# Half-size PSUM tiles, a reordered stage schedule and a fixed matmul order in a long FFT convolution

## The chip, the cores and the metric

The kernel runs on one core of one Trainium2 chip. The metric is device time in microseconds (us), here of that one core. Each kernel was run several times; medians of those runs are quoted, and a ratio comes with a 95% interval. A run is called *slow* when it is over 1.5% above the fastest run of the same kernel, else *fast*; ratios use fast runs only. A time is about 1.8 us longer than the span that the profile of the same run shows (396.82 us and 395.0 us for the kernel before).

Names of engines: PE is the matrix engine, ACT the scalar engine, DVE the vector engine, POOL the general-purpose one, SP the one that mostly issues DMAs. PSUM is the memory that matmuls write into; an *eviction* is the instruction, here on ACT or DVE, that reads a PSUM tile and so frees it. The *granted clock* of PE is the share of its full clock that the profile shows as granted: 1.00 is full, and PE is called *cold* where it is near 0.5 and *warm* where it is near 1.

## The reference

```python
x = A_q
g = sigmoid((x * gate_w).sum(-1, keepdims=True))
# branch a: 4-tap shift convolution of k, times v, then a long convolution by FFT
kv = k_shift * v                                   # S=2048, D=640
y  = irfft(rfft(pad(kv)) * rfft(pad(ssm_k)))[:S]   # padded to 4096
a  = q * (y + kv * ssm_D)
# branch b: sliding attention, 32 heads of 20, 8 keys at a distance of 2, then @ wo
out = g * a + (1 - g) * b
```

## The kernel before: the parts that matter

The kernel does three things one after the other: projections, attention (branch b, which leaves `(1-g)*b` in a scratch buffer), and the FFT stage (branch a). The change touches the last two. The FFTs are written as matmuls with constant matrices, in two steps each way, and the 160 channels of a partition are worked through in four groups, `g` = 0 to 3:

| stage | PE writes | who evicts, into what |
|---|---|---|
| `u_s1`, `h_s1` | 10 small or 5 large `pa` tiles each | ACT casts to `Am` |
| `h_s2` | 6 `pb` tiles | DVE adds `Dg`, giving `Hs`; then two copies give `Hsw` |
| `u_s2` | 6 `pb` tiles | ACT casts to `Up`; then two large DVE products `Vp = Up*Hsw`, `Up = Up*Hs` |
| `inv_s1` | `pa` tiles | ACT casts to `Cm` |
| `inv_s2` | `pa` tiles | DVE multiplies into `a_lin`; POOL adds `b_lin` |

```python
pp = tile_pool(name="af_ps", bufs=2, space=PSUM)
...
# after the loads of the FFT stage: one large multiply
nc.vector.tensor_tensor(a_lin[:], a_lin[:], g_lin[:].unsqueeze(2).to_broadcast([128, 64, 160]), ALU.mult)
...
def s1_stage(X_lin, g):
    ...
        nil = min(4, IL - il0)
        pa = pp.tile([128, 2, 512], F32, name="pa", tag="pa")      # 1024 columns, ring of 2
        for l in range(nil): nc.tensor.matmul(pa[...], lhsT=X_lin[...], rhs=F1bd[:, :], ...)
        evac(Am[:, :, :, :, il0:il0 + nil], src)                   # nc.scalar.copy
...
fwd_u_s1(0)
fwd_h(0)                                                           # h_s1 and h_s2
fwd_u_s2(0)
for g in range(NG):
    if g + 1 < NG: fwd_u_s1(g + 1)
    inv_s1(g)
    if g + 1 < NG: fwd_h(g + 1)
    inv_s2(g)
    if g + 1 < NG: fwd_u_s2(g + 1)
```

When the kernel is built, a scheduler orders the instructions of each engine by readiness, unless instructions carry an *issue-order token*: those with the same token keep the order in which they were written. The kernel before has no such token in its FFT stage, and what it executes is not what is written: in the group that is read below, PE's `inv_s2` matmuls begin at 311.9 us, before the first one of `h_s2` (312.9), and are then spread among them, although `inv_s2(g)` is called after `fwd_h(g + 1)`.

The softmax here doesn't subtract the row's maximum and nothing guards it: scores larger than these inputs give would overflow.

## Time and profile before

| | us |
|---|---|
| median of 4 runs when the prediction was made | 392.98 (390.76 to 396.82) |
| projections, to | 124 |
| attention, to | 233 |
| FFT stage, to the end of the span | 395 |

First the page of the profile: busy time, share of the span, and instructions of each engine. No engine is full over the whole span, but the three parts have different limits, so this line decides nothing.

```profile
PE 265.1 (67%) x3958; PEld 181.3 (46%) x3958; DVE 244.4 (62%) x304; ACT 179.2 (45%) x230; POOL 101.7 (26%) x102
```

The view of windows divides the FFT stage at the ends of the `Up` products of groups 1 to 3. Columns: window, its length, busy time and instructions of PE, weight loads, DVE, ACT, POOL; then the granted PE clock, the DMA share and GB/s.

```profile
262.80:299.30 36.50, 23.70 (x504) 20.05 (x504) 30.28 (x17) 19.02 (x22) 12.08 (x6) 0.87 0.51 111
299.30:333.50 34.20, 23.56 (x504) 20.09 (x504) 19.90 (x17) 19.12 (x22) 12.34 (x7) 0.90 0.01 2
...
367.80:395.00 27.20, 10.78 (x208) 10.20 (x208) 3.24 (x6) 4.93 (x6) 10.36 (x13) 0.69 0.42 98
```

In the steady group of 34.20 us PE is busy for 23.56, DVE for 19.90, ACT for 19.12. No engine is full there either. What does fill the group is seen in the chain of waits: the work that ended last, followed backwards. Columns: start, duration, what (a cut of that same group).

```profile
295.68 3.63 DVE Up L256
...
302.99 1.02 ACT Cm L191
...
308.12 3.77 ACT Am L191 x4
313.50 4.35 DVE Hs L236 x4
...
318.41 1.46 DVE Hs L236 x2
...
320.47 1.49 DVE Hsw L239
321.97 2.31 DVE Hsw L240
...
326.33 3.60 DVE Vp L255
329.95 3.63 DVE Up L256
```

From one `Up` product (ends at 299.3) to the next (333.5) the chain passes through inverse stage 1, the `Am` of h, the `Hs` adds, the copies to `Hsw`, and the two products. The engines take turns.

At the start of the stage stands the large multiply of `a_lin`. DVE's timeline (start, duration, engine, line, operation, tiles, count):

```profile
268.62 10.83 DVE L178 TENSOR_TENSOR a_lin<-a_lin,g_lin 128x10240 bf16<-128x10240 bf16 x1 [5.83 <-DMA a_lin<-in_A_q_dram]
279.36 2.21 DVE L236 TENSOR_TENSOR Hs<-pb,Dg 128x960 bf16<-128x960 f32 x2
281.49 0.65 DVE L299 TENSOR_TENSOR a_lin<-pa,a_lin 128x480 bf16<-128x480 f32 x1
...
295.68 3.62 DVE L256 TENSOR_TENSOR Up<-Up,Hs 128x5120 bf16<-128x5120 bf16 x1
```

It starts when its load lands and runs ahead of all `Hs` adds of group 1. In attention, the line that the change moves to another engine is this group (busy, mean ns of one, idle before):

```profile
L419 DVE TENSOR_SCALAR fin<-op,omg 128x640 bf16<-128x640 f32 x16 | 14.1, 881 | 7.4 <-PE op L416 7.2
```

### The profile page before, as it was taken

The numbers are of one execution on the slowest core, as the hardware profiler recorded it, in microseconds if no ns is written. First come the engines' busy times: TensorE is split into PE (matmuls) and PEld (weight loads), VectorE is DVE, ScalarE is ACT, GpSimd is POOL, SyncE is SP. The second block draws the span as 40 slices with busy tenths as digits, with TensorE's granted clock in tenths as the row PEclk, the third lists the DMA queues.
The fourth block names the chain that finished last, engine by engine and source line by source line (L and its number), as shares of the span: only waits on it lengthen the run. The fifth ranks groups of instructions, "written<-read, shape, count | busy, mean of one in ns | idle before, by whom it ended". The sixth has DMA issues, their size and how long they took to land.

```text
span 395.0 us, 8971 instructions
## 1 busy us (share of the span) xinstructions
PE 265.1 (67%) x3958; PEld 181.3 (46%) x3958; DVE 244.4 (62%) x304; ACT 179.2 (45%) x230; POOL 101.7 (26%) x102
## 2 busy tenths in 40 slices
PE   0599999749541787786968566656666774772730
PEld 0365555324130555465545334545556563672630
DVE  0241095899689879788687623558993297079230
ACT  1025545423371747657374236648084644823310
POOL 5019702091003600000000043000263048017263
PEclk9999999987855559597577989669896998898695
DMA  8935998583351911010000149999300000000037
GB/s 230 264 98 95 161 189 174 114 151 66 76 135 35 201 34 51 2 51 22 33 18 20 50 134 266 298 198 286 45 2 2 2 3 2 0 3 2 2 78 189
DMA packets 26375, 37.36 MB, mean 95 GB/s; under 512 B 15424, under 2 KB 21204, under 8 KB 25824
## 3 DMA queue, kind: packets, MB, share of 16 engines
q1 hardware_dynamic: 21104, 19.62, 20.7%
q0 software_dynamic: 5232, 17.17, 20.0%
q8 instruction: 31, 0.51, 0.5%
q14 instruction: 8, 0.07, 0.1%
HBM read 26.26 MB, written 5.25 MB: 80 GB/s over the span
## 4 chain that ended last, share of the span: by engine, by line
PE 22%; DVE 18%; ACT 10%; SPq 6%; issue 5%; DMA 2%; POOL 2%; POOLq 0%; ACTq 0%; DVEq 0%
PE op L416 7%; SPq L176 6%; ACT ET L453 6%; PE sc L447 4%; DVE Hs L236 4%; PE O L469 4%; DVE Up L256 3%; DVE Vp L255 3%; DMA a_lin<-in_A_q_dram 2%; ACT Cm L191 2%; PE pa L270 2%; DVE a_lin L299 2%; ACT Am L191 2%; PE tr L488 2%; PE pa L272 2%
## 5 line engine op out<-in xcount | busy, mean ns | idle before, releaser
L453 ACT ACTIVATE ET<-sc 128x912 bf16<-128x912 f32 (+1 forms) x80 | 64.1, 854 | 49.2 <-PE sc L447 38.1
L300 POOL TENSOR_TENSOR a_lin<-a_lin,b_lin 128x480 bf16<-128x480 bf16 (+1 forms) x24 | 43.2, 1819 | 97.4 <-DVE a_lin L299 97.4
L369 PE MATMUL pj<-xT,W 128*128 128x512 bf16 x200 | 49.8, 405 | 10.3 <-ACT stg L372 10.3
L454 DVE TENSOR_TENSOR ET<-ET,band 128x912 bf16<-128x912 bf16 (+1 forms) x80 | 45.2, 567 | 8.7 <-ACT ET L453 7.9
L191 ACT CAST Am<-pa 128x1024 bf16<-128x1024 f32 x40 | 37.4, 1039 | 18.4 <-PE pa L201 12.9
L447 PE MATMUL sc<-q,k 20*128 20x114 bf16 x576 | 31.0, 252 | 20.9 <-ACT ET L453 20.0
L270 PE MATMUL pa<-MU,Up 128*128 128x128 bf16 x160 | 28.0, 270 | 21.8 <-DVE Up L256 19.9
L236 DVE TENSOR_TENSOR Hs<-pb,Dg 128x960 bf16<-128x960 f32 (+1 forms) x24 | 23.6, 1036 | 30.4 <-PE pb L221 30.4
L219 PE MATMUL pb<-Am,Gre 64*128 64x80 bf16 x512 | 26.5, 208 | 15.2 <-DVE Hs L236 7.1
L369 PEld LDWEIGHTS <-W 128*128 128x128 bf16 x200 | 20.2, 102 | 35.6 <-issue 15.8
L372 ACT CAST stg<-pj 128x512 bf16<-128x512 f32 x40 | 22.6, 588 | 30.5 <-PE pj L369 18.9
L416 PE MATMUL op<-wo,oT 128*128 128x512 bf16 (+1 forms) x160 | 33.1, 362 | 3.0 <-DVE fin L419 3.0
L191 ACT CAST Cm<-pa 128x1024 bf16<-128x1024 f32 (+1 forms) x24 | 19.7, 875 | 29.5 <-PE pa L272 29.5
L253 ACT CAST Up<-pb 128x960 bf16<-128x960 f32 (+1 forms) x24 | 19.3, 886 | 29.7 <-issue 27.5
L469 PE MATMUL O<-VW,ET 128*128 128x21 bf16 x576 | 21.8, 177 | 13.0 <-DVE o_S L478 12.6
L221 PEld LDWEIGHTS <-Gim 64*128 64x128 bf16 x512 | 22.3, 102 | 17.5 <-issue 17.2
L270 PEld LDWEIGHTS <-Up 128*128 128x128 bf16 x160 | 20.3, 127 | 20.9 <-DVE Up L256 12.2
L399 ACT CAST VW<-psv 128x640 bf16<-128x640 f32 x18 | 12.6, 699 | 37.3 <-PE psv L397 37.3
L447 PEld LDWEIGHTS <-k 20*128 20x128 bf16 x576 | 16.6, 106 | 25.4 <-issue 20.5
L272 PE MATMUL pa<-MV,Vp 128*128 128x128 bf16 x160 | 28.1, 271 | 0.0
L469 PEld LDWEIGHTS <-ET 128*128 128x128 bf16 x576 | 19.1, 101 | 17.3 <-issue 12.9
L221 PE MATMUL pb<-Am,Gim 64*128 64x80 bf16 x512 | 26.7, 208 | 0.0
(75 smaller groups left out, 490.9 us busy)
## 6 DMA issues: line engine op xcount, KB each, us to landing
h_lin<-in_A_v_dram POOLq DMA_DIRECT2D x4, 640.0 KB, 16.3
h_lin<-in_A_ssm_k_dram POOLq DMA_DIRECT2D x8, 320.0 KB, 6.3
b_scr<-fin SPq DMA_DIRECT2D x16, 160.0 KB
W<-in_B_wqkv_dram SPq DMA_DIRECT2D x3, 800.0 KB
kh<-in_A_k_dram POOLq DMA_DIRECT2D x12, 190.0 KB, 13.9
q<-stg SPq DMA_DIRECT2D x28, 80.0 KB
k<-stg SPq DMA_DIRECT2D x28, 80.0 KB
Him<-ca_Him POOLq DMA_DIRECT2D x1, 2048.0 KB, 19.0
```

The lines of the kernel that those rows point to most:

```text
L191: nc.scalar.copy(dst, src)
L221: nc.tensor.matmul(o, lhsT=Gim[rows, j1, :], rhs=Am[rows, j1, 1, :, :].rearrange("p q l -> p (q l)"), start=False, stop=True, tile_positio ...
L236: nc.vector.tensor_tensor(Hs[:, :, :, j0:j0 + nj, :], view, Dgv.unsqueeze(3).to_broadcast([128, 2, IL, nj, 4]), ALU.add)
L270: nc.tensor.matmul(o, lhsT=Up[:, c2, il, :, :].rearrange("p j q -> p (j q)"), rhs=MU[:, :], start=True, stop=False, skip_group_check=True)
L272: nc.tensor.matmul(o, lhsT=Vp[:, c2, il, :, :].rearrange("p j q -> p (j q)"), rhs=MV[:, :], start=False, stop=True, skip_group_check=True)
L300: nc.gpsimd.tensor_tensor(reg, reg, breg, ALU.add)
L369: nc.tensor.matmul(ps[:], lhsT=W[:, dt, which, 128 * ft:128 * ft + 128], rhs=xT[:, dt, HALO + 512 * sc:HALO + 512 * sc + 512], start=(dt = ...
L416: nc.tensor.matmul(op[:, n0:n1], lhsT=oT[:, ft, HALO + 128 * sb:HALO + 128 * sb + 128], rhs=wo[:, ft, n0:n1], start=(ft == 0), stop=(ft == ...
L447: nc.tensor.matmul(sc[:, hh, bb * BP:bb * BP + BP], lhsT=k32[32 * h4:32 * h4 + DH, t, kc:kc + 128], rhs=q32[32 * h4:32 * h4 + DH, t, qc:qc ...
L453: nc.scalar.activation(dst, src, ACT.Exp, scale=SCALE)
L454: nc.vector.tensor_tensor(dst, dst, band[:].unsqueeze(1).unsqueeze(1).to_broadcast([128, 2, nbb, BP]), ALU.mult)
L469: nc.tensor.matmul(O[:, slot * 21:slot * 21 + 21], lhsT=ET[:, h4, bb, :], rhs=VW[:, b, h, :], start=True, stop=True, skip_group_check=True)
```

## The change

The intent is a deeper pipeline: more and smaller PSUM tiles, so that evictions start sooner, and the transform of h one group ahead, so that `Hsw` is ready when `Up` needs it. Five things change:

1. `pa` tiles have 512 columns and a ring of four (four buffers that are used in turn), instead of 1024 and two.
2. The stages are called in another order.
3. Every matmul of the FFT stage carries one issue-order token, so PE executes them as written.
4. In the last group the adds of `b_lin` run on DVE, and the output is stored at rows 24, 48, 60 and 64, the last store from ACT's queue too.
5. `fin` in attention moves from DVE to ACT.

```diff
+        def mm(*args, **kwargs):
+            inst = nc.tensor.matmul(*args, **kwargs)
+            tc.stamp_issue_order_token(inst.ins, "fft_pe")
+            return inst
 ...
-                nil = min(4, IL - il0)
-                pa = pp.tile([128, 2, 512], F32, name="pa", tag="pa")
+                nil = min(2, IL - il0)
+                pa = pp.tile([128, 512], F32, name="pa", tag="pa", bufs=4)
 ...                                  # the same in inv_s1 and inv_s2; all matmuls become mm(...)
-                    nc.gpsimd.tensor_tensor(reg, reg, breg, ALU.add)
+                    (nc.vector if g == NG - 1 else nc.gpsimd).tensor_tensor(reg, reg, breg, ALU.add)
 ...
-        fwd_u_s1(0)
-        fwd_h(0)
-        fwd_u_s2(0)
+        fwd_u_s1(0); fwd_h_s1(0); fwd_h_s2(0); fwd_u_s2(0)
+        if NG > 1:
+            fwd_u_s1(1); fwd_h_s1(1); fwd_h_s2(1)
         for g in range(NG):
-            if g + 1 < NG:
-                fwd_u_s1(g + 1)
             inv_s1(g)
             if g + 1 < NG:
-                fwd_h(g + 1)
+                fwd_u_s2(g + 1)
             inv_s2(g)
-            if g + 1 < NG:
-                fwd_u_s2(g + 1)
+            if g + 2 < NG:
+                fwd_u_s1(g + 2); fwd_h_s1(g + 2); fwd_h_s2(g + 2)
 ...
-            nc.vector.tensor_scalar(fin[:], op[:, 0:D], omg[:, sb:sb + 1], None, ALU.mult)
+            nc.scalar.activation(fin[:], op[:, 0:D], ACT.Copy, scale=omg[:, sb:sb + 1])
```

More of the change, by code (lines that the diff above doesn't have):

```diff
@@ L196, in s1_stage @@
             while il0 < IL:
-                nil = min(4, IL - il0)
-                pa = pp.tile([128, 2, 512], F32, name="pa", tag="pa")
+                nil = min(2, IL - il0)
+                pa = pp.tile([128, 512], F32, name="pa", tag="pa", bufs=4)
                 for l in range(nil):
                     i = IL * g + il0 + l
-                    nc.tensor.matmul(pa[:, l // 2, 256 * (l % 2):256 * (l % 2) + 256],
+                    mm(pa[:, 256 * l:256 * l + 256],
                                      lhsT=X_lin[:, i, :, :].rearrange("p c n -> p (c n)"), rhs=F1bd[:, :],
                                      start=True, stop=True, skip_group_check=True)
-                src = pa[:].rearrange("p b (w m) -> p (b w) m", w=2)[:, 0:nil, :].rearrange("p l (q j r) -> p j r q l", q=4, j=32)
+                src = pa[:, 0:256 * nil].rearrange("p (l q j r) -> p j r q l", l=nil, q=4, j=32)
                 evac(Am[:, :, :, :, il0:il0 + nil], src)
@@ L218, in s2_stage @@
                         o = pb[:, c2, 80 * jj:80 * jj + 80]
-                        nc.tensor.matmul(o, lhsT=Gre[rows, j1, :], rhs=Am[rows, j1, 0, :, :].rearrange("p q l -> p (q l)"),
+                        mm(o, lhsT=Gre[rows, j1, :], rhs=Am[rows, j1, 0, :, :].rearrange("p q l -> p (q l)"),
                                          start=True, stop=False, tile_position=(64 * c2, 0), skip_group_check=True)
-                        nc.tensor.matmul(o, lhsT=Gim[rows, j1, :], rhs=Am[rows, j1, 1, :, :].rearrange("p q l -> p (q l)"),
+                        mm(o, lhsT=Gim[rows, j1, :], rhs=Am[rows, j1, 1, :, :].rearrange("p q l -> p (q l)"),
                                          start=False, stop=True, tile_position=(64 * c2, 0), skip_group_check=True)
@@ L227, in a_fft, with fwd_h_s1, fwd_h_s2 @@
         st = {}
-        def fwd_h(g):
-            Am_h = s1_stage(h_lin, g)
+        def fwd_h_s1(g):
+            st[("Amh", g)] = s1_stage(h_lin, g)
+        def fwd_h_s2(g):
+            Am_h = st.pop(("Amh", g))
             Hs = pl.tile([128, 2, IL, 32, 4], BF, name="Hs", tag="Hs")
@@ L264, in inv_s1 @@
                 while il0 < IL:
-                    nil = min(8, IL - il0)
-                    pa = pp.tile([128, 2, 512], F32, name="pa", tag="pa")
+                    nil = min(4, IL - il0)
+                    pa = pp.tile([128, 512], F32, name="pa", tag="pa", bufs=4)
                     for l in range(nil):
                         il = il0 + l
-                        o = pa[:, l // 4, 128 * (l % 4):128 * (l % 4) + 128]
-                        nc.tensor.matmul(o, lhsT=Up[:, c2, il, :, :].rearrange("p j q -> p (j q)"), rhs=MU[:, :],
+                        o = pa[:, 128 * l:128 * l + 128]
+                        mm(o, lhsT=Up[:, c2, il, :, :].rearrange("p j q -> p (j q)"), rhs=MU[:, :],
                                          start=True, stop=False, skip_group_check=True)
-                        nc.tensor.matmul(o, lhsT=Vp[:, c2, il, :, :].rearrange("p j q -> p (j q)"), rhs=MV[:, :],
+                        mm(o, lhsT=Vp[:, c2, il, :, :].rearrange("p j q -> p (j q)"), rhs=MV[:, :],
                                          start=False, stop=True, skip_group_check=True)
-                    src = pa[:].rearrange("p b (w m) -> p (b w) m", w=4)[:, 0:nil, :].rearrange("p l (n r) -> p n r l", r=2)
+                    src = pa[:, 0:128 * nil].rearrange("p (l n r) -> p n r l", l=nil, r=2)
                     evac(Cm[:, :, :, c2, il0:il0 + nil], src)
@@ L284, in inv_s2 @@
             while n0 < 64:
-                nn = min(24, 64 - n0)
-                pa = pp.tile([128, 2, 512], F32, name="pa", tag="pa")
+                nn = min(12, 64 - n0)
+                pa = pp.tile([128, 512], F32, name="pa", tag="pa", bufs=4)
                 for k_ in range(nn):
                     n2 = n0 + k_
-                    o = pa[:, k_ // 12, 40 * (k_ % 12):40 * (k_ % 12) + 40]
-                    nc.tensor.matmul(o, lhsT=Hre[:, n2, :], rhs=Cm[:, n2, 0, :, :].rearrange("p c l -> p (c l)"),
+                    o = pa[:, 40 * k_:40 * k_ + 40]
+                    mm(o, lhsT=Hre[:, n2, :], rhs=Cm[:, n2, 0, :, :].rearrange("p c l -> p (c l)"),
@@ L291, in inv_s2 @@
                                      start=True, stop=False, skip_group_check=True)
-                    nc.tensor.matmul(o, lhsT=Him[:, n2, :], rhs=Cm[:, n2, 1, :, :].rearrange("p c l -> p (c l)"),
+                    mm(o, lhsT=Him[:, n2, :], rhs=Cm[:, n2, 1, :, :].rearrange("p c l -> p (c l)"),
                                      start=False, stop=True, skip_group_check=True)
-                for bq in range((nn + 11) // 12):
-                    m = min(12, nn - 12 * bq)
-                    yv = pa[:, bq, 0:40 * m].rearrange("p (n c l) -> p n c l", n=m, c=2)
-                    reg = a4[:, n0 + 12 * bq:n0 + 12 * bq + m, :, IL * g:IL * g + IL]
-                    breg = b4[:, n0 + 12 * bq:n0 + 12 * bq + m, :, IL * g:IL * g + IL]
+                if True:
+                    m = nn
+                    yv = pa[:, 0:40 * m].rearrange("p (n c l) -> p n c l", n=m, c=2)
+                    reg = a4[:, n0:n0 + m, :, IL * g:IL * g + IL]
+                    breg = b4[:, n0:n0 + m, :, IL * g:IL * g + IL]
@@ L299, in inv_s2 @@
                     nc.vector.tensor_tensor(reg, yv, reg, ALU.mult)
-                    nc.gpsimd.tensor_tensor(reg, reg, breg, ALU.add)
-                if g == NG - 1:
+                    (nc.vector if g == NG - 1 else nc.gpsimd).tensor_tensor(reg, reg, breg, ALU.add)
+                n0 += nn
+                if g == NG - 1 and n0 in (24, 48, 60, 64):
+                    w0 = {24: 0, 48: 24, 60: 48, 64: 60}[n0]
                     for cq in range(4):
-                        eng = (nc.sync, nc.gpsimd)[cq % 2]
-                        dst = outf[:, 160 * cq:160 * cq + 160].rearrange("(a b) c -> a b c", b=64)[:, n0:n0 + nn, :]
-                        eng.dma_start(dst, a_lin[32 * cq:32 * cq + 32, n0:n0 + nn, :])
@@ L306, in inv_s2 @@
-                n0 += nn
-        fwd_u_s1(0)
-        fwd_h(0)
-        fwd_u_s2(0)
+                        eng = (nc.sync, nc.gpsimd, nc.scalar)[cq % 3] if n0 == 64 else (nc.sync, nc.gpsimd)[cq % 2]
+                        dst = outf[:, 160 * cq:160 * cq + 160].rearrange("(a b) c -> a b c", b=64)[:, w0:n0, :]
+                        eng.dma_start(dst, a_lin[32 * cq:32 * cq + 32, w0:n0, :])
+        fwd_u_s1(0); fwd_h_s1(0); fwd_h_s2(0); fwd_u_s2(0)
+        if NG > 1:
+            fwd_u_s1(1); fwd_h_s1(1); fwd_h_s2(1)
```

## The prediction

> **What bounds it now.** The span (395.0 us, one profiled run of 396.82 against a median of 392.98) has three parts: projection to 124 us, attention to 233, the FFT stage to 395. The change touches the last two. By the windows view no engine is full in the FFT stage: from 299.3 to 333.5 PE is busy 23.6 of 34.2 us, DVE 19.9, ACT 19.1. The chain of waits shows why: one group is a serial chain that repeats every 34.2 us (Up products end at 299.3, 333.5, 367.8): inverse stage 1 on a PE that restarts at half clock 7.6; four or five Am evictions 5.2; Hs adds, Hsw copies and a_lin multiplies on DVE about 13; Vp and Up 7.2; handoffs.
>
> **What the change does.** The instruction order shows PE work pinned in program order; no matmul is added or removed.
> - Evictions of 128x1024 become 128x512. The trace has 1039 ns against 599. The Trainium skill (ScalarE: Activation LUTs, "What ACT_TABLE_LOAD costs") gives 186 ns + 0.833 per element, overlapping by 93: 0.52 us per 512 against 0.95, and the trace agrees (0.92 between starts). Ten Am tiles (9.3 us) become twenty (10.4); Cm 4.9 becomes 5.2. ACT pays about 1.4 us a group.
> - A ring of four small tiles instead of two large lets the first eviction start earlier, 0.4 us per stage.
> - New order: h is transformed a group ahead, so Hsw leaves the chain. But u and h evictions now run back to back inside it, and their PSUM tiles wait for a_lin multiplies, which DVE runs only after Vp and Up. New chain per group, walked by hand: Am 10.4, Hs until PE may go on 4.5, Cm 5.8, Up evictions 4.9, a_lin/Vp/Up 8.3, handoffs 0.8: about 34.7 against 34.2. **The pipeline is relabelled, not shortened.**
> - Start: the a_lin load lands at 268.6 and the 10.8 us DVE multiply after it now stands behind three Hs adds of group 1 and holds up PE, which has inverse stage 1 of group 0 still to do. I expect Up of group 1 about 3 us later.
> - Tail: 512-wide tiles bring the first last-group multiply about 0.9 us sooner after Up; the adds move from POOL (1.1 us each, plus handoff) to DVE (estimated 0.33 from 2.82 us per 5120 elements). But 2.6 MB of output at the 230 GB/s seen takes 11 us, so the end follows the first store: gain 1 to 2 us.
> - fin (883 ns on DVE, 16 times) becomes an ACT activation, estimated 0.81 us (same page, pointer scale). Where op, fin, op alternate, DVE is full (2.8 us per step against 2.2 without fin), so attention may gain 1 to 4 us.
>
> **Sum.** FFT stage +1 to +4 from order and eviction overhead, tail -1 to -2, attention -1 to -4: about -2.5 us, 390.5 us. Range 383 to 397. Chances: faster by 2% 0.22, within 2% 0.70, slower 0.08.
>
> **What would show it.** Time between ends of Up products: 33 to 36 us if right; 30 or less if stages overlap better than I think. ACT should idle 7 to 9 us per group, waiting on PE behind a_lin. The large a_lin multiply should start near 270 minus any attention gain. PE should begin inverse stage 1 warm in groups 1 and 2 (54 ns between matmuls, not 105; skill, TensorE: Matmul & The Clock Gate, "What's actually happening"). Attention windows should be 105 to 108 us instead of 109.
>
> **What would make it wrong.** PE staying cold through the eviction-bound stages (+2 us a group); POOL adds no longer colliding with Vp and Up (3.6 against 2.8 us), which would save up to 1.5 us a group; ACT, about 60% busy in attention, delaying exp behind fin; the output DMA ending sooner.

## The result and the profile after

| | before | after |
|---|---|---|
| median, us | 393.76 (16 runs, 390.76 to 399.39) | 402.79 (11 runs, 400.11 to 406.46) |
| ratio of fast runs | | 1.0225 [1.0186, 1.0263] |
| profiled run: span, mean clock | 395.0, 0.825 | 401.0, 0.786 |

The ratio is the mean time of one kernel's fast runs over the mean of the other's fast runs of the same rounds, so it is not quite the ratio of the two medians. The changed kernel is slower by 2.25%, which is 8.9 us of the 393.76; that it is slower is clear of the noise, that it is slower by 2% is not, as the interval reaches down to 1.0186. The time lies outside the predicted range.

The profile of before fell in a run called slow, for being over 1.5% above the fastest run. So the kernel before was profiled once more, later (run before_again, below; a single run). Its FFT stage agrees with the first profile: 34.0 and 34.1 us between `Up` products against 34.2 and 34.3. In the comparison by stage I use before_again.

| us after the last `fin` (end of attention) | before_again | after | after takes longer by |
|---|---|---|---|
| end of the `Up` product of group 0 | 29.3 | 30.0 | 0.7 |
| of group 1 | 66.2 | 69.9 | 3.7 so far |
| group 1 to 2 | 34.0 | 35.5 | 1.5 |
| group 2 to 3 | 34.1 | 36.1 | 2.0 |
| group 3 to the first output store | 12.9 | 11.0 | -1.9 |
| first store to the end | 14.6 | 15.7 | 1.1 |
| end | 161.7 | 168.2 | 6.5 |
| length of attention | 106.7 | 107.5 | 0.8 |

Attention is counted here from the start of its first `o_S` multiply on DVE to the end of the last `fin`. So 6.5 of the 8.9 us are placed in the FFT stage. The rest is not placed: in this pair of profiles, whose spans differ by 8.3 us, it is 0.8 us of attention and 1.1 us before it, and both are within the scatter. The projection part, which no kernel touches, ends anywhere between 123.0 and 126.8 us in the sixteen profiles, and attention between 106.3 and 107.5 us later; a single pair of profiles can't resolve 2 us there.

The page of after and its windows, cut at the same events. The steady group has grown from 34.20 to 35.60 and 36.10 us although DVE has less to do, ACT only a little more and PE the same matmuls, and the granted clock is 0.79 and 0.78 instead of 0.90 and 0.85.

```profile
PE 274.6 (68%) x3958; PEld 183.8 (46%) x3958; DVE 228.6 (57%) x294; ACT 194.7 (49%) x302; POOL 92.2 (23%) x97
```

```profile
262.80:302.60 39.80, 20.20 (x476) 17.52 (x476) 26.63 (x15) 14.41 (x25) 6.24 (x2) 0.72 0.48 101
302.60:338.20 35.60, 25.16 (x504) 20.08 (x504) 18.05 (x18) 19.97 (x36) 11.05 (x7) 0.79 0.01 2
338.20:374.30 36.10, 25.82 (x504) 20.65 (x503) 17.84 (x17) 20.24 (x36) 10.94 (x7) 0.78 0.01 2
374.30:401.00 26.70, 10.19 (x208) 10.02 (x208) 6.82 (x16) 5.42 (x10) 9.23 (x12) 0.69 0.45 100
```

The chain of waits of this trace reaches back only to 382.5 us, so the group has to be read from timelines. ACT's, where the bracket is the idle time before the instruction and what ended it:

```profile
290.86 4.83 ACT L261 CAST Up<-pb 128x960 bf16<-128x960 f32 x6
303.95 1.12 ACT L196 CAST Am<-pa 128x512 bf16<-128x512 f32 x2 [8.27 <-PE pa L190]
305.24 9.20 ACT L196 CAST Am<-pa 128x512 bf16<-128x512 f32 x18 [0.17 <-PE pa L190]
321.54 4.99 ACT L196 CAST Cm<-pa 128x512 bf16<-128x512 f32 x10 [7.10 <-PE pa L190]
326.32 4.87 ACT L261 CAST Up<-pb 128x960 bf16<-128x960 f32 x6
```

This is the whole group on one engine. All `Am` together take 10.49 us (303.95 to 314.44), then ACT waits 7.10, `Cm` takes 4.78 until the first `Up`, `Up` takes 4.87, and then it waits 8.27 again before the next group. The sum is 35.5 us, the measured distance between groups. The group is a serial chain again, with two holes. DVE's timeline shows what stands in them:

```profile
268.36 3.39 DVE L244 TENSOR_TENSOR Hs<-pb,Dg 128x960 bf16<-128x960 f32 x3 [5.53 <-PE pb L190]
271.66 10.81 DVE L178 TENSOR_TENSOR a_lin<-a_lin,g_lin 128x10240 bf16<-128x10240 bf16 x1
282.40 2.61 DVE L244 TENSOR_TENSOR Hs<-pb,Dg 128x960 bf16<-128x960 f32 x3
...
296.19 2.81 DVE L263 TENSOR_TENSOR Vp<-Up,Hsw 128x5120 bf16<-128x5120 bf16 x1
...
299.49 3.17 DVE L264 TENSOR_TENSOR Up<-Up,Hs 128x5120 bf16<-128x5120 bf16 x1
302.58 2.00 DVE L307 TENSOR_TENSOR a_lin<-pa,a_lin 128x480 bf16<-128x480 f32 x4
```

- The hole of 8.27 us: after the last `Up` eviction DVE does the two long products and only then most of the `a_lin` multiplies, which free the `pa` tiles of `inv_s2`. PE has `u_s1` of the next group behind them in its fixed order, so ACT gets its first `Am` of the next group only at 303.95 us, when the last run of `a_lin` multiplies (from 302.58) has begun to free tiles.
- The hole of 7.10 us: PE is in `h_s2`, where ACT has nothing to do, and `inv_s1`, which would give ACT its `Cm` work, is written after it.
- At the start, the large multiply has slipped behind three of the six `Hs` adds. While it runs, two of the other three `pb` tiles stand full and PE waits 10.81 us to write the sixth (the line below); `inv_s1` of group 0 is written after `h_s2` of group 1, and the first `Cm` comes at 285.06 us, after ACT has been idle for 17.78.

```profile
283.60 0.25 PE L190 MATMUL pb<-Am,Gre 64*128 64x80 bf16 x2 [10.81 <-DVE Hs L244]
```

The PE clock in the same group, from the windows between the events on ACT (`Am`; from `Am` to `Cm`; `Cm`):

```profile
303.95:314.45 10.50, 7.58 (x38) 4.39 (x37) 0.63 (x2) 10.33 (x20) 3.35 (x4) 0.82 0.01 2
314.45:321.50 7.05, 6.21 (x140) 5.46 (x140) 5.96 (x6) 0.00 (x0) 0.00 (x0) 0.52 0.01 2
321.50:326.30 4.80, 4.80 (x120) 4.70 (x118) 3.02 (x3) 4.76 (x10) 0.00 (x0) 1.00 0.00 0
```

`h_s2` runs at a clock of 0.52; just before it PE, which waits for evictions there, had a pause of 1.6 us. `inv_s1` begins cold too, at 320.42 us: its first ten matmuls stand 105 ns apart, the later ones 55 ns. While ACT evicts `Cm`, the clock is 1.00 in this group. In the next group 32 matmuls of `inv_s1` stand 105 ns apart.

In attention, `fin` is now on ACT and takes 793 ns:

```profile
L426 ACT ACTIVATE fin<-op,omg 128x640 bf16<-128x640 f32 x16 | 12.7, 793 | 28.1 <-PE op L423 19.2 <-issue 6.5 <-ACT ET L460 2.4
```

### The profile page after: what moved, and what is told of

It is laid out like the page before. It is cut to its first block, busy times and chain, and to the rows that moved or that the text cites. A ratio compares the mean times of both kernels' runs of the same rounds, so it can differ in the third digit from the quotient of the medians.

```text
span 401.0 us, 9049 instructions
## 1 busy us (share of the span) xinstructions
PE 274.6 (68%) x3958; PEld 183.8 (46%) x3958; DVE 228.6 (57%) x294; ACT 194.7 (49%) x302; POOL 92.2 (23%) x97
## 5 line engine op out<-in xcount | busy, mean ns | idle before, releaser
L376 PE MATMUL pj<-xT,W 128*128 128x512 bf16 x200 | 49.2, 401 | 10.8 <-ACT stg L379 10.8
L308 POOL TENSOR_TENSOR a_lin<-a_lin,b_lin 128x480 bf16<-128x480 bf16 (+1 forms) x18 | 32.8, 1854 | 102.5 <-DVE a_lin L307 102.5
L190 PE MATMUL pb<-Am,Gre 64*128 64x80 bf16 x512 | 32.6, 233 | 27.1 <-DVE Hs L244 14.7
L196 ACT CAST Am<-pa 128x512 bf16<-128x512 f32 x80 | 41.1, 728 | 17.5 <-PE pa L190 17.5
L190 PEld LDWEIGHTS <-Gim 64*128 64x128 bf16 x512 | 27.9, 119 | 31.8 <-issue 31.7
L196 ACT CAST Cm<-pa 128x512 bf16<-128x512 f32 x40 | 21.0, 613 | 42.8 <-PE pa L190 42.8
L190 PE MATMUL pb<-Am,Gim 64*128 64x80 bf16 x512 | 33.2, 235 | 0.1
L307 DVE TENSOR_TENSOR a_lin<-pa,a_lin 128x480 bf16<-128x480 f32 (+1 forms) x24 | 13.3, 591 | 28.9 <-PE pa L190 28.9
L190 PEld LDWEIGHTS <-Gre 64*128 64x128 bf16 x512 | 28.7, 119 | 1.1 <-issue 0.8
L476 PEld LDWEIGHTS <-ET 128*128 128x128 bf16 x576 | 19.2, 102 | 18.2 <-issue 12.7
L426 ACT ACTIVATE fin<-op,omg 128x640 bf16<-128x640 f32 x16 | 12.7, 793 | 28.1 <-PE op L423 19.2
L190 PE MATMUL pa<-MU,Up 128*128 128x128 bf16 x160 | 24.0, 252 | 3.3 <-DVE a_lin L307 3.3
```

Of the source, the lines that this page charges most:

```text
L190: inst = nc.tensor.matmul(*args, **kwargs)
L196: nc.scalar.copy(dst, src)
L307: nc.vector.tensor_tensor(reg, yv, reg, ALU.mult)
L308: (nc.vector if g == NG - 1 else nc.gpsimd).tensor_tensor(reg, reg, breg, ALU.add)
L376: nc.tensor.matmul(ps[:], lhsT=W[:, dt, which, 128 * ft:128 * ft + 128], rhs=xT[:, dt, HALO + 512 * sc:HALO + 512 * sc + 512], start=(dt = ...
L476: nc.tensor.matmul(O[:, slot * 21:slot * 21 + 21], lhsT=ET[:, h4, bb, :], rhs=VW[:, b, h, :], start=True, stop=True, skip_group_check=True)
```

## The experiments

My theory after this reading: the loss comes from the order that PE is held to, because it lines up waits that another order overlaps (the two holes and the start). The rivals: (a) twice as many evictions cost ACT more than the deeper ring gives; (b) the token itself costs something, whatever the order; (c) the change of `fin` or of the tail is to blame. All kernels below gave correct results. Ratios are to the kernel before in the same batch (medians there 394.7, 395.63, 395.24 and 396.77 us).

### The parts that are not the order

**before_again**: the kernel before, unchanged, for a second profile.

> The unchanged kernel, only to get a trace of it in the fast state, since the profile of before fell in the slow state at 395.0 us. All theories: a span of 389 to 393 us. If the 4 us between this and the 395.0 sit in the matrix engine's half-clock stretches, the FFT windows shrink; if in attention or projection, those do.

Measured: 394.58 us, span 392.7 us; used in the table above.

**before_fin_act**: only `fin` moves to ACT, in the kernel before.

```diff
-            nc.vector.tensor_scalar(fin[:], op[:, 0:D], omg[:, sb:sb + 1], None, ALU.mult)
+            nc.scalar.activation(fin[:], op[:, 0:D], ACT.Copy, scale=omg[:, sb:sb + 1])
```

> Before, with the fin scaling alone moved from DVE to ACT. Theory one (the loss is the FFT stage's new order): ratio 0.997 to 1.004, attention window 108 to 109 us, because the after profile already shows attention ending within 0.3 us of before. Rival (ACT, in order, makes exp wait for fin and this costs several us hidden by the slow state of the before profile): ratio 1.008 or more.

Measured: 1.0028 [0.9981, 1.0075]. Attention takes 107.2 us, against 106.7 in before_again. The move neither costs nor gains anything that these runs resolve; the gain of 1 to 4 us that I predicted isn't there. (The interval does leave room for a cost of up to 0.75%, about 3 us.) In the waits view of attention, ACT's wait for the score matmuls (`ET` behind `sc`, 37.6 us in before) gave way in after to waits of `fin` for the output projection (19.2 us): the wait moved along with `fin`. PE's output projection (`op`), which waits for the `fin` of an earlier block, shows it; engine and what it waited for, us in total, times, longest, first before, then after:

```profile
PE op L416 <- DVE fin L419: 3.0, 6, 1.0
```

```profile
PE op L423 <- ACT fin L426: 3.2, 8, 0.9
```

**before_small_tiles**: only the tiles, in the kernel before.

```diff
-                nil = min(4, IL - il0)
-                pa = pp.tile([128, 2, 512], F32, name="pa", tag="pa")
+                nil = min(2, IL - il0)
+                pa = pp.tile([128, 512], F32, name="pa", tag="pa", bufs=4)
 ...                  # likewise in inv_s1 (8 -> 4) and inv_s2 (24 -> 12), store points kept
```

> Before, with the tiles alone changed (512 columns, ring of four), old stage order, scheduler free. Theory one: the extra 1.4 us of eviction per group is mostly hidden by the earlier start, ratio 0.995 to 1.010. Rival (the fixed cost of twice as many evictions is the loss): ratio 1.018 or more, with 1.5 us or more added to each group's 34.2 us.

Measured: 391.91 us, 0.9941 [0.9879, 1.0003]. Groups take 31.4 and 31.1 us instead of 34.0 and 34.1. So rival (a) has the wrong sign in this order: the small tiles shorten a group by almost 3 us, although ACT has more instructions.

**after_big_tiles**: the reverse, large tiles in the kernel after.

```diff
-                pa = pp.tile([128, 512], F32, name="pa", tag="pa", bufs=4)
+                pa = pp.tile([128, 1024], F32, name="pa", tag="pa", bufs=2)
 ...                  # with 4, 8 and 24 columns' worth per tile again, stores at 24, 48, 64
```

> After, with the tiles alone put back to 1024 columns in a ring of two; new order, pinned PE and fin on ACT stay. Theory one: still slow, ratio to before 1.012 to 1.03, ACT still idle 7 us or more per group while PE waits on a_lin behind Vp and Up. Rival (eviction cost): ratio 1.005 or less.

Measured: 396.99 us, 1.0062 [1.0011, 1.0113], between what the theory and the rival said. The groups are as long as in after, or longer (36.3 and 36.8 us; ACT idle 9.04 us in the first hole). What is better is the start: `Up` of group 1 ends at 61.8 us instead of 69.9. In this build the large multiply happened to fall behind four `Hs` adds instead of three. With two `pb` buffers that lets PE write the last two tiles, and it begins `inv_s1` of group 0 at 269.9 us, during the multiply; in after it begins at 284.0, behind it. The run therefore doesn't speak for eviction cost, and it raised the next question: how much hangs on the place of that one DVE instruction?

**after_old_tail**: the tail of before (adds on POOL, two queues, stores at 24, 48, 64) in the kernel after.

```diff
-                    (nc.vector if g == NG - 1 else nc.gpsimd).tensor_tensor(reg, reg, breg, ALU.add)
+                    nc.gpsimd.tensor_tensor(reg, reg, breg, ALU.add)
-                if g == NG - 1 and n0 in (24, 48, 60, 64):
+                if g == NG - 1 and n0 in (24, 48, 64):
```

> After with the old end: adds of the last group on POOL, stores of 24, 24 and 16 rows from two queues. From the profiles, after starts its first store 11.0 us after the last Up product and ends 15.7 us later, before 12.9 and 14.6. Theory: what the earlier store gains the smaller last stores give back; within 1.5 us of after, ratio to before 1.018 to 1.027. Rival (the new tail loses, or gains, 3 us or more): outside 1.015 to 1.030.

Measured: 401.21 us, 1.0192 [1.0108, 1.0276], which overlaps the interval of after. From the last `Up` product to the end it took 26.3 us (141.4 to 167.7) against 26.7 (141.5 to 168.2) in after. The new tail gains nothing of its own: its first store goes out earlier and the rest takes longer. As the main cause, rival (c) is out in both its halves; that `fin` adds a part of the 2.4 us that are not placed is not excluded.

### The order, freed

**after_free_order**: the kernel after without the token. One line goes; nothing else is changed.

```diff
         def mm(*args, **kwargs):
             inst = nc.tensor.matmul(*args, **kwargs)
-            tc.stamp_issue_order_token(inst.ins, "fft_pe")
             return inst
```

> After without the pin on the matrix engine's order; nothing else. The scheduler now pulls group 1's evictions and inverse stage 1 forward and puts the large a_lin multiply after all six Hs adds. Theory (pinned order holds inverse stage 1 of group 0 behind the large multiply): first Up products after the last fin end at about 60 to 64 us instead of 69.9, groups after that 33 to 35.5 us, ratio to before 0.995 to 1.008. Rival (small tiles in this order are slow whatever the pin): ratio 1.015 or more.

Measured: 384.04 us, 0.9724 [0.9682, 0.9765], groups of 32.5 us and `Up` of group 1 at 59.5 us instead of 69.9. One line turns 2.25% slower into 2.8% faster. All three values lie beyond what I had expected, on the fast side. A caution: in this build DVE's order changed as well. The large multiply now stands behind all six `Hs` adds of group 1 (it starts at 270.87 us), and that place alone, with PE still pinned, is worth 7.5 of the 10.4 us at the start (after_mul_late, below). The groups are not touched by it; they show what the matmul order does. ACT's timeline for one group:

```profile
294.37 9.21 ACT L195 CAST Am<-pa 128x512 bf16<-128x512 f32 x18 [0.17 <-PE pa L190]
303.21 1.33 ACT L195 CAST Cm<-pa 128x512 bf16<-128x512 f32 x2
304.87 0.58 ACT L195 CAST Cm<-pa 128x512 bf16<-128x512 f32 x1 [0.33 <-PE pa L190]
...
309.59 3.03 ACT L195 CAST Cm<-pa 128x512 bf16<-128x512 f32 x6 [0.58 <-PE pa L190]
312.45 4.82 ACT L260 CAST Up<-pb 128x960 bf16<-128x960 f32 x6
```

The scheduler has mixed `inv_s1` into `h_s2`: the first four `Cm` evictions run just before or during the `Hs` adds. From the end of `Am` to the first `Up` it takes 8.9 us (303.58 to 312.45) instead of 11.9 (314.44 to 326.32). That difference of 3.0 us is what a group lost (35.5 to 32.5). The second hole is closed in part, by order alone.

**pinned_like_free**: pinned again, but written in nearly the order that the scheduler had found: some `u_s1(1)` tiles among those of `u_s2(0)`, three `inv_s1` tiles before `h_s2` and two between its tiles; the large multiply is placed after the `Hs` adds of group 1 and held there by a token on DVE.

```diff
+            inv = inv_s1_tiles(g)                    # inv_s1 as a generator, one step per tile
+            if g + 1 < NG:
+                run(inv, 3 if g else 0)
+                fwd_h_s2(g + 1, inv)                 # two steps of inv after each pb tile
 ...
+            run(inv)
             if g + 1 < NG:
                 fwd_u_s2(g + 1)
             inv_s2(g)
             if g + 2 < NG:
-                fwd_u_s1(g + 2); fwd_h_s1(g + 2); fwd_h_s2(g + 2)
+                fwd_u_s1(g + 2); fwd_h_s1(g + 2)
```

> After with PE still pinned, but the program written in nearly the order that the scheduler chose when it was free: u evictions of group 1 pulled into forward stage 2 of u of group 0, inverse stage 1 of the previous group spread between the tiles of forward stage 2 of h, the large multiply behind six Hs adds. If what the pin costs is only the order as written: ratio to before 0.968 to 0.980, Up of group 1 at 58 to 62 us after the last fin, groups 32 to 33.5 us. If the pin costs by itself (waits, overhead): ratio 1.00 or more, groups 35 us or more.

Measured: 388.57 us, 0.9795 [0.9733, 0.9858], groups of 32.5 and 31.9 us. Every FFT matmul carries the token, and the groups are as short as without it. Rival (b) falls: it isn't the token that costs, it is the order that it makes binding. (The start is slower than in the free kernel, 63.6 us to `Up` of group 1 against 59.5, and misses the 58 to 62 that I had expected; my copy of the order was not exact there.)

**before_small_pin**: the stage order of before, with small tiles and the token: written order, executed as written.

```diff
+        def mm(*args, **kwargs):
+            inst = nc.tensor.matmul(*args, **kwargs)
+            tc.stamp_issue_order_token(inst.ins, "fft_pe")
+            return inst
 ...                  # before_small_tiles, with mm(...) for every FFT matmul
```

> Before's stage order with small tiles, matmul order pinned: the fourth corner to small tiles free (0.994), new order free (0.972) and new order pinned (1.0225). Theory (the pin hurts because the new order as written puts Hs adds and Cm evictions one behind the other): in the old order, which the scheduler had left almost as written, the pin costs 0 to 1.2%, ratio 0.994 to 1.006. Rival (pinning costs by itself, as an overhead of every matmul or wait): ratio 1.03 or more.

Measured: 403.55 us, 1.0233 [1.0164, 1.0302]. I had expected at most 1.2% for it, and that fell. The same kernel without the token has 0.9941, so pinning costs the *old* order 2.9% as well: its groups go from 31.4 to 37.2 us. ACT's wait before the `Up` evictions shows where, first pinned, then free:

```profile
326.64 1.82 ACT L257 CAST Up<-pb 128x960 bf16<-128x960 f32 x2 [13.52 <-issue]
```

```profile
321.04 4.74 ACT L253 CAST Up<-pb 128x960 bf16<-128x960 f32 x6 [7.63 <-issue]
```

PE's order says what ACT waits for. Free, the `inv_s2` matmuls begin at 311.9 us and are mixed with those of `h_s2`, and `u_s2`, which feeds `Up`, begins at 320.3. Pinned, `h_s2` runs from 313.2 us, `inv_s2` only behind it from 319.1, and `u_s2` from 325.7.

So the two stage orders, pinned, are equal (1.0225 and 1.0233). Freed, the new one is better in total (0.9724 against 0.9941; `fin` and the tail differ there too, but moved nothing that their own runs could resolve), and only by its start: `Up` of group 1 ends at 59.5 us against 67.6, with the large multiply behind six `Hs` adds in one build and before all of them in the other. The groups of the new order are longer (32.5 us against 31.4 and 31.1). What pinning an order as written costs by itself is seen in the groups: 3.0 and 3.6 us in the new order, 5.9 and 6.0 in the old.

### The start and the first hole

**after_mul_late**: one DVE instruction moved. The large multiply is emitted after the six `Hs` adds of group 1, and the `Hs` adds and the multiply carry a DVE token so that it stays there.

```diff
-        nc.vector.tensor_tensor(a_lin[:], a_lin[:], g_lin[:].unsqueeze(2).to_broadcast([128, 64, 160]), ALU.mult)
 ...
             fwd_u_s1(1); fwd_h_s1(1); fwd_h_s2(1)
+            vt(a_lin[:], a_lin[:], g_lin[:].unsqueeze(2).to_broadcast([128, 64, 160]), ALU.mult)
```

> After, with one change of order on DVE: the large a_lin multiply stands behind six Hs adds of group 1 instead of three; PE order stays pinned. Theory: PE runs inverse stage 1 of group 0 during the multiply, so Up of group 1 ends about 62 us after the last fin instead of 69.9, and the end moves by the same 7 to 8 us: ratio to before 1.000 to 1.006, groups 2 and 3 unchanged at 35 to 36.5 us. Rival (the start is not what costs): ratio 1.015 or more.

Measured: 393.96 us, 0.9975 [0.9929, 1.0021]. `Up` of group 1 ends at 62.4 us instead of 69.9; the groups stay at 35.5 and 36.6. DVE's timeline:

```profile
265.42 6.02 DVE L193 TENSOR_TENSOR Hs<-pb,Dg 128x960 bf16<-128x960 f32 x6 [5.56 <-PE pb L189]
271.36 10.82 DVE L193 TENSOR_TENSOR a_lin<-a_lin,g_lin 128x10240 bf16<-128x10240 bf16 x1
...
285.80 2.81 DVE L266 TENSOR_TENSOR Vp<-Up,Hsw 128x5120 bf16<-128x5120 bf16 x1
```

The multiply starts at almost the same moment as in after (271.36 and 271.66 us of the two spans), but now all six `pb` tiles are free before it. PE runs on into `inv_s1` and `u_s2`, ACT evicts `Cm` from 271.39 us, and `Vp` begins at 285.80. In after, `Cm` began at 285.06 and `Vp` at 296.19. The place of one instruction was worth 7.5 us.

**after_products_late**: the two products `Vp` and `Up` are emitted after `inv_s2` instead of inside `u_s2`, with all DVE work of the stage in written order.

```diff
             s2_stage(Am_u, consume_u)
-            nc.vector.tensor_tensor(Vp[:], Up[:], Hsw[:], ALU.mult)
-            nc.vector.tensor_tensor(Up[:], Up[:], Hs[:], ALU.mult)
+            st[("UH", g)] = (Up, Vp, Hs, Hsw)        # products now in fwd_u_mul(g)
 ...
             inv_s2(g)
+            if g + 1 < NG:
+                fwd_u_mul(g + 1)
```

> After, with Vp and Up of the next group put behind the six a_lin multiplies on DVE (order pinned there too); the large multiply stays where it was. Theory (PE waits for PSUM tiles whose a_lin multiply stands behind Vp and Up): the 8.3 us idle stretch of ACT before the Am evictions shrinks to 1 to 2.5 us and each group from 35.8 to 28 to 30 us; ratio to before 0.985 to 0.997. Rival (ACT's twenty evictions bound the group): no less than 34 us per group and ratio over 1.01.

Measured: 395.76 us, 1.0011 [0.9961, 1.0061]. The groups shrink to 30.5 and 30.9 us, and ACT's wait for its first `Am` from 8.27 to 2.85 us:

```profile
326.73 10.28 ACT L204 CAST Am<-pa 128x512 bf16<-128x512 f32 x20 [2.85 <-PE pa L190]
```

So the first hole was the products standing in front of the `a_lin` multiplies: 5.4 us of wait gone, 5.0 to 5.2 us of group gone. That is a little less than I had expected (1 to 2.5 us of wait left, groups of 28 to 30, a ratio of 0.985 to 0.997). The start got worse (73.1 us to `Up` of group 1, against 69.9), since the products there now wait for all of `inv_s2(0)`. That hides 3 of the 10 us gained.

**after_both_late**: both, the large multiply just before `inv_s2(0)`.

```diff
+            if g == 0:
+                vt(a_lin[:], a_lin[:], g_lin[:].unsqueeze(2).to_broadcast([128, 64, 160]), ALU.mult)
             inv_s2(g)
+            if g + 1 < NG:
+                fwd_u_mul(g + 1)
```

> Both moves at once: products behind the a_lin multiplies, and the large multiply behind group 1's Hs and Hsw. If the two losses are separate they add: first Up of group 1 at 64 to 68 us after the last fin (the multiply now precedes the a_lin multiplies there), groups 28 to 30 us, ratio to before 0.970 to 0.985, faster than both kernels. If they overlap, no better than the product move alone by more than 2 us.

Measured: 387.41 us, 0.981 [0.9763, 0.9857]; groups 30.1 and 30.4 us, `Up` of group 1 at 65.3 us. PE is still pinned exactly as in the change. Two moves on DVE alone bring the kernel from 2.25% above to 1.9% below.

### All of it together

**interleaved**: both DVE moves (the multiply before the `Hsw` copies), and PE pinned with two `inv_s1` tiles written between the `pb` tiles of `h_s2`.

```diff
-                fwd_u_s1(g + 2); fwd_h_s1(g + 2); fwd_h_s2(g + 2)
+                fwd_u_s1(g + 2); fwd_h_s1(g + 2); fwd_h_s2(g + 2, inv_s1_tiles(g + 1))
```

> Built on the earlier results: both moves of DVE order (large multiply behind six Hs adds, products behind the a_lin multiplies), and the pinned PE order itself rewritten so that inverse stage 1 of the previous group stands between the tiles of forward stage 2 of h. Theory (what the pin costs is that Cm evictions on ACT can't run beside Hs adds on DVE): groups 23 to 27 us, Up of group 1 about 63 us after the last fin, ratio to before 0.935 to 0.955. Rival (the gain of the free order came from somewhere else, such as the start): groups stay at 30 us and the ratio at 0.97 or more.

Measured: 387.91 us, 0.9834 [0.9775, 0.9893]. A miss on all counts that I had set: a ratio of 0.935 to 0.955, groups of 23 to 27 us, where 28.8 and 28.1 were measured, and a start of about 63 us, where it took 69.9. For the start I would argue that nothing pulls the `Am` work of group 1 forward in this pinned order; no run tests that.

**free_both_late**: both DVE moves, and PE free.

```diff
-            tc.stamp_issue_order_token(inst.ins, "fft_pe")      # in mm(), with the edits of
 ...                                                             # after_products_late, and:
             s2_stage(Am_h, consume_h)
+            if g == 1:
+                vt(a_lin[:], a_lin[:], g_lin[:].unsqueeze(2).to_broadcast([128, 64, 160]), ALU.mult)
```

> The same two moves on DVE, PE order left to the scheduler. Theory: the gains of the free order (0.972) and of the moves (0.981 pinned) add in part; Up of group 1 at 60 to 64 us, groups 27 to 30 us, ratio to before 0.955 to 0.970. If the scheduler's own order already had both, 0.972 as before.

Measured: 377.57 us, 0.9573 [0.9512, 0.9634], the fastest; it beats both kernels. Groups of 26.7 and 26.8 us, `Up` of group 1 at 62.7 us. ACT's timeline for one group, and the same group as a window:

```profile
315.55 10.31 ACT L202 CAST Am<-pa 128x512 bf16<-128x512 f32 x20 [2.85 <-PE pa L189]
325.46 1.36 ACT L202 CAST Cm<-pa 128x512 bf16<-128x512 f32 x2
...
331.87 3.03 ACT L202 CAST Cm<-pa 128x512 bf16<-128x512 f32 x6 [0.58 <-PE pa L189]
334.74 4.82 ACT L269 CAST Up<-pb 128x960 bf16<-128x960 f32 x6
```

```profile
303.90:330.60 26.70, 21.78 (x504) 17.09 (x504) 18.94 (x17) 20.08 (x36) 11.03 (x6) 1.00 0.01 3
```

ACT has the same 20 us of work as in after (20.08 against 19.97), in a group that is 8.9 us shorter, and PE is granted its full clock throughout this window.

**after_kept_warm**: to separate the half clock in `h_s2` from the missing overlap, the stage-1 matmuls were done twice, so that PE would have no pause before `h_s2`.

```diff
+                    for _rep in range(2):
                         mm(pa[:, 256 * l:256 * l + 256], ...)
```

> After with every stage 1 forward matmul issued twice (same result, PE busier while ACT evicts Am), nothing else. If the half clock in forward stage 2 of h and inverse stage 1 is most of the group's extra 3 us against the free order (trace: 0.50 granted from 314.7 to 320.7 us): groups 32.5 to 34 us and ratio to before 1.005 to 1.015. If the lost overlap of Cm evictions with Hs adds is most of it: groups 34.7 to 36 us, ratio 1.017 to 1.03.

Measured: 404.52 us, 1.0184 [1.0129, 1.024], groups of 37.6 us. As a test of the total it is inconclusive: the doubled matmuls began on a cold PE and slowed the first `Am` evictions themselves (the first four stand about 0.85 us apart), so the test brought a cost of its own; nor did PE stay warm (0.67 from 314 to 320 us).

The traces narrow the question all the same. In after_kept_warm `h_s2` at least begins warm (its first pairs of matmuls stand 0.035 us apart, in after 0.066). From the end of `Am` to the first `Hs` add it then takes 0.69 us, as in the free kernel, and 1.08 in after. The six adds take 6.02 us, as in after; in the free kernel 5.81. So the last add ends 7.10 us after `Am` in after and 6.50 in the free kernel. From there to the first `Up` eviction it takes 4.78 us and 2.37, because four of the ten `Cm` are done by then in the free kernel. By this reading of one group, some 2.4 of the 3.0 us are the missing overlap, and the half clock in `h_s2` is worth 0.6 at most. No run isolates it.

## Why the prediction was wrong

**Point by point.**

- *What bounds the kernel* was right. A serial chain over three engines sets the time of a group, before and after, and no engine is full.
- *ACT idles 7 to 9 us per group behind `a_lin`* was right (8.27 us), and so was its cause (after_products_late).
- *The large multiply stands behind three `Hs` adds of group 1 and holds up PE*: right, including the time near 270 us (271.66). I said 3 us for it; `Up` of group 1 came 3.7 us later.
- *The steady group takes 34.7 us, "relabelled, not shortened"*: it took 35.5 and 36.1. The terms taken from durations held: `Am` 10.4 predicted and 10.49 measured, `Up` 4.9 and 4.87, a_lin/Vp/Up 8.3 and 8.27. The term that was mis-sized is "Hs until PE may go on 4.5": from the end of `Am` (314.44 us) to the first matmul of `inv_s1` (320.42) it took 5.98 us, and 5.60 in the next group. The first add starts 1.08 us after `Am`, the adds take 1.0 us each, and PE's last tile has to wait for four of them. "Cm 5.8", from there to the first `Up` eviction, took 5.90 and 6.93. With "handoffs 0.8", the three together were 11.1 predicted, 11.9 and 12.5 measured.
- *PE warm at inverse stage 1* was wrong in both groups named: ten matmuls stand 105 ns apart in one and 32 in the other. I had named a cold PE only among what would make it wrong.
- *Attention gains 1 to 4 us* was wrong. It gains nothing (before_fin_act). I counted what DVE would be relieved of, at a place where the profile showed DVE full, without asking what would wait for `fin` on its new engine: PE waited 3.0 us in all for DVE's `fin` before, and 3.2 for ACT's after.
- *The tail gains 1 to 2 us*: 0.8 us from the last `Up` product to the end (27.5 in before_again, 26.7 in after), and the old tail does as well in the new kernel.

**The sum.** My own terms for the FFT stage, 3 for the start and 0.5 for each of two groups, make +4, the upper end of the "+1 to +4" that I then wrote. With the two gains that did not come it led to -2.5 us. The measured terms are +3.7, +1.5, +2.0 and -0.8 with attention at about zero, +6.4 in all, which is the 6.5 of the table but for rounding. The remaining 2.4 us of the difference of 8.9 are not placed.

**The steps that failed**, in the terms of the prediction, are these. "Attention -1 to -4": measured, no gain. "Hs until PE may go on 4.5": 5.98 and 5.60, so that the groups grew by 1.5 and 2.0 us and not by 0.5. And "FFT stage +1 to +4" was written lower than its own terms, which make the +4.

**Behind the second** stands a question that was not asked. "The instruction order shows PE work pinned in program order" stands in the prediction as a fact, before the list of costs. I walked the pinned order, but never against the order that the scheduler would have chosen. The kernel before looked, in its source, as if it ran its stages in order too. It didn't: its order was the scheduler's. The change therefore took away an overlap that nobody had written down. By the experiments the pin is the largest single term: from 1.0225 to 0.9724 by freeing the order (with the place of the large multiply in it, see above), and from 0.9941 to 1.0233 by pinning the old one. This says why the changed kernel is slow. It does not by itself say why my sum was off, since the chain of 34.7 us was that of the pinned order.

The Trainium skill says what makes this hard, in "TensorE: Matmul & The Clock Gate", section "Step-by-step: what each phase is for": "The MATMULs themselves stay in program order". The traces agree: in after, `Cm` work that could have run during the 7.10 us hole begins only when `h_s2` is through, as the order was written.

On the smaller side of the ledger, the costs per instruction from the skill held. "ScalarE: Activation LUTs", section "What ACT_TABLE_LOAD costs", gives 93 ns for a scale that is read through a pointer; `fin` took 793 ns, and a copy of the same 128x640 shape without one 699 (698 in after), a difference of 94 to 95. The evictions were costed rightly, and the rival that they would lose is refuted by before_small_tiles, in the old order.

## What to carry to other kernels

Before costing a change that fixes an order, compare the order that is executed now with the one that will be; where a scheduler mixed stages, pinning them as written takes that overlap away, and reordering can only be judged with and without the pin. Walk the chain on one engine as a sum of its work and its holes (here 20.1 us of work and 15.4 of holes on ACT in a group of 35.5), and ask of each hole which instruction on which queue stands in front. A long instruction whose own result is not needed yet, like the 10.8 us multiply, does its harm by where it stands in the queue: behind three adds or behind six made 7.5 us to the end of the next `Up` product.

## What the Trainium skill lacked or had wrong

- "TensorE: Matmul & The Clock Gate", section "What's actually happening", has PE go cold after an idle window of about 3.4 us. In after PE was granted 1.00 from 308.7 to 312.7 us (busy 2.99 of 4.0), was busy 0.37 of the next 2.0 us with one pause of 1.6 us, and had a clock of 0.50 from 314.7 us. A shorter pause, after a stretch of part-time work, was enough here. (Another section of that page, "A second HAM failure mode: psum-queue depth-cycling", does have short pauses between groups of matmuls bring the clock down, but gives no length for them.)
- "Perfetto Trace Analysis", section "Optimization Strategy", says that the same gap repeating may mean too few or too small buffers. Here a gap of 8.27 us repeated in each group; with the other tile size and ring it was 9.04 us, and moving two DVE products behind other instructions made it 2.85. No page that I found speaks of the cost of a fixed program order across stages; it was 3.0 and 3.6 us in groups of 35.5 and 36.1 us here.
- "SBUF — State Buffer", section "Who interferes with whom", calls the port that DVE shares with GpSimd an exclusive lock for the whole instruction. It gives no size for a mixture like this one: the `Up` product took 2.82 us in group 0, and 3.62 in a later group of before, where adds of `b_lin` run on POOL.
